# Attention and top-1 experts on one core: token lists by comparisons and matmuls in place of scatters, and the first expert slot begun beside the last attention pair

## The chip, the cores and the metric

The kernel runs on one core of one Trainium2 chip. The metric is the device time of one execution in microseconds; before and after are compared by the median of their runs. The engines are called PE (matmuls), DVE (vector), ACT (scalar), POOL (GpSimd) and SP (its queue issues most of the loads). Each works through its own queue of instructions in the order in which the program issues them.

## The reference, cut to what matters

```python
q_rot, k_rot = (rotate(q), rotate(k))                  # 8 batches, 8 heads, 576 tokens, 64 wide
scores = scale * np.matmul(q_rot, k_rot.transpose(0, 1, 3, 2))
attn = softmax(scores)
x = (attn @ v).transpose(0, 2, 1, 3).reshape(4608, 512)
logits = x @ w_gate
e_idx = np.argmax(logits, axis=1)                      # one of 8 experts for each token
gate_w = softmax(logits)[np.arange(N), e_idx]
eom = 1.0 / (1.0 + np.exp(-(x @ w_output_gate)))
for e in range(8):
    mask = e_idx == e
    h = np.maximum(x[mask] @ w1[e], 0.0)               # 512 x 1024
    out[mask] = gate_w[mask, None] * eom[mask, e, None] * (h @ w2[e])
```

Which token goes to which expert is known only when the attention of the token has been computed, so the kernel makes lists of tokens for each expert as it runs and gathers the rows by them.

## The kernel before, in words

**Attention.** 32 pairs of heads (8 batches, 4 pairs each), 9 steps a pair, 288 steps. In a step (`Attention.step`) PE computes the scores of 128 queries in one of two PSUM tiles (`scores`, lines 432 and 439), DVE takes the row maximum (`peak`, 445), ACT the exponential (`exp`, 454), and one step later DVE transposes it in blocks of 32 (`turn`, 460). Everything else of a pair is issued at fixed steps by the list `EVENTS`: the load of the next pair's q and k on SP (`load`), the rotation on POOL (`mult`, 388, and `add`, 392), the split into a high and a low part on ACT and POOL (364, 372), the value products on PE in four pieces (`values`, 479) in steps 2, 4, 6 and 8 of the next pair, then `evict` on ACT (486 to 488), `back` on PE (494), which turns the rows to tokens and computes the gates' logits, and `divide` on DVE and ACT (502 to 511), which writes a tile `xb` of the batch. So each `evict` (line 486) ends a pair's work on PE.

**Placing a batch.** `place` returns a list of small pieces, issued one a step from step 36b+47 on for batch b. The small arithmetic is on POOL for all batches but the last, for which it is on DVE. The pieces choose the expert (s0 to s8), compute the gate (s9 to s12), store the rows to a DRAM tensor `xd` by SP (s13), compute each token's place in its expert's list by two small matmuls (s14, lines 599 and 600; their PSUM tile is borrowed from the score tiles), and round it to an integer (s17, 612). Then five pieces each issue an indirect DMA from POOL (`scatter`, 616), which writes 128 token numbers, 4 bytes each, to one of five list tensors in DRAM. These five are filled with a large number at the start.

**Tables.** `table0`, `table1` (two tables) turn the counts of tokens into a list of slots; each ends in `slots`, which gathers list rows from the five list tensors by five indirect DMAs on POOL (706), some pieces later takes the minimum of the five on DVE (713), transposes it on PE (717) and rounds it to indices (718). The first table counts the tokens of batches 0 to 5 only. Its pieces begin at `att.done(nb - 3) + 1`; `nplace` is there the length of the last batch's list of pieces, 23, so that step is 251, and the gather falls among batch 5's scatters. `fetch` gathers the rows of slots 0 and 1 (832); its tile shares the buffers of `xb`.

**The passage.** After step 287 the pools of the rotation are closed and the first four weight loads are issued (`begin0`). After one more step the score tiles are closed and two PSUM banks (`ps_x`) take small tiles. The rest of the events up to step 296 follows (the last pair's value products, line 479, and `evict`), then `begin1`: the split of the first weights (`split`, 854 and 856), the transposes of the gathered rows (`turn`, 870 to 873), two more splits. Then the last `back` and `divide`. Only then is the attention's PSUM closed and `ps_m` opened with four tags: `ph0`, `ph1` for the first products, `py0`, `py1` for the second.

**Experts.** 14 slots of 256 tokens and 12 of 128 (`todo`): 5 by the first table, 9 and 12 by the second and third. A slot has eight parts: four times `first` (products with w1, lines 888 and 898) and four times `second` (926). In each, weights six parts ahead are split, weights eight parts ahead are loaded, and two of the pieces `left` are issued: the last batch's placing, merged with the second and third table's. `store` scatters the result (938), `gather` fetches rows (832), both on POOL's queue.

## Time and profile before

| | |
|---|---|
| median of three runs | 1230.01 us (1220.46, 1232.24, 1230.01) |
| the profiled execution | 1221.57 us, its span 1219.8 us |
| granted TensorE clock, mean | 0.924 |
| busy: PE | 1074.2 us, 88% |
| busy: DVE, ACT, POOL | 835.0, 640.2, 597.9 us |
| first `evict` (line 486), last | 54.1 us, 709.2 us |
| indirect scatters of the lists | 40, mean 1040 ns on POOL |

The profile is of one execution. Busy times are sums over the span. A row of a group of instructions has its line, engine and operation, the tile written and the tile read, the shapes and the count, then busy time and mean ns of one, then the idle time of its engine just before, with the instruction that ended it. In the timeline a row has its start, its length, and in brackets the idle time before it with the releaser; "issue" there is time in which the engine waited for nothing that the profile shows. The granted clock is 1.00 at full speed and 0.50 at half.

### The profile page before, as it was taken

Reading aid. Unit: us, or ns where it says so; the run is one execution under the profiler, and the core shown is the slowest. Engines: PE = TensorE matmul, PEld = TensorE weight load, DVE = VectorE, ACT = ScalarE, POOL = GpSimd, SP = SyncE. Lnnn points to the kernel's source line nnn. Section 1 sums busy time; section 2 is a strip of 40 time slices with the busy share of each in tenths; the row PEclk is TensorE's granted clock in tenths of the full one; section 3 lists DMA queues with packets and bytes.
Section 4 is the critical chain, followed back from the end, with each engine's and each line's share of the span. In section 5 each row is a group of like instructions: output and inputs, shape, how many; then the busy total and the mean of one; then the engine's idle time right before and its main releaser. Section 6 shows DMA issues by size and latency. Waiting matters only on the chain.

```text
span 1219.8 us, 34628 instructions
## 1 busy us (share of the span) xinstructions
PE 1074.2 (88%) x14419; PEld 919.9 (75%) x14419; DVE 835.0 (68%) x1335; ACT 640.2 (52%) x1309; POOL 597.9 (49%) x535
## 2 busy tenths in 40 slices
PE   3999985999887888989857879989999999999998
PEld 2877764777766766777646578878988989889986
DVE  6788863876765766767747347655677786786784
ACT  3566642554543544545424245433576675686573
POOL 4676765566774675575554312332154253353242
PEclk9999987988987998878868869989999999999999
DMA  6544486484675675574724647956578788797791
GB/s 206 157 143 134 120 165 80 111 164 112 153 126 86 159 113 140 131 126 110 162 36 79 213 139 210 239 191 214 185 253 301 266 298 278 272 330 263 269 338 40
DMA packets 55713, 216.87 MB, mean 178 GB/s; under 512 B 10337, under 2 KB 11260, under 8 KB 47488
## 3 DMA queue, kind: packets, MB, share of 16 engines
q1 hardware_dynamic: 46432, 194.77, 59.0%
q0 software_dynamic: 8160, 19.03, 4.6%
q8 instruction: 115, 1.88, 0.7%
q10 hardware_dynamic: 960, 0.82, 0.2%
q14 instruction: 46, 0.38, 0.1%
HBM read 195.98 MB, written 20.70 MB: 178 GB/s over the span
## 4 chain that ended last, share of the span: by engine, by line
PE 65%; DVE 12%; issue 9%; DMA 5%; ACT 4%; another core or an unknown queue 2%; POOL 2%; SPq 0%; POOLq 0%; ACTq 0%; DVEq 0%
PE py L926 15%; PE acc L479 14%; PE sc L439 14%; PE ph L898 12%; PE ph L888 4%; DVE pt L460 3%; DVE m L445 3%; PE sc L432 3%; DMA wr<-in_w 2%; PE acc L494 2%; ACT pm L454 2%; DVE wl L856 1%; PE mtp L870 1%; DMA lst<-tok,pi 1%
## 5 line engine op out<-in xcount | busy, mean ns | idle before, releaser
L454 ACT ACTIVATE pm<-sc,m 128x576 f32<-128x576 f32 x288 | 213.2, 740 | 283.1 <-DVE m L445 281.3
L445 DVE TENSOR_REDUCE m<-sc 128x1 f32<-128x576 f32 x288 | 213.7, 742 | 171.2 <-PE sc L439 156.0
L856 DVE TENSOR_TENSOR wl<-wr,wh 128x1024 fp32r<-128x1024 f32 x183 | 252.2, 1389 | 68.3 <-ACT wh L854 66.3
L479 PE MATMUL acc<-pt,v 32*64 32x160 f32 (+1 forms) x9216 | 240.1, 322 | 58.1 <-issue 33.0
L439 PE MATMUL sc<-kh,q 64*128 64x288 f32 x1024 | 239.9, 345 | 54.3 <-ACT pm L454 39.5
L479 PEld LDWEIGHTS acc<-pt,v 32*64 32x64 f32 x9216 | 184.0, 145 | 97.3 <-issue 65.0
L439 PEld LDWEIGHTS sc<-kh,q 64*128 64x128 f32 x1024 | 164.1, 207 | 103.3 <-ACT pm L454 55.8
L460 DVE STREAM_TRANSPOSE pt<-pm 128x576 f32<-128x576 f32 x288 | 220.5, 766 | 12.5 <-ACT pm L454 11.6
L854 ACT CAST wh<-wr 128x1024 fp32r<-128x1024 f32 x208 | 213.1, 1051 | 4.5 <-DMA wr<-in_w 4.4
L926 PE MATMUL py<-wh,ht 128*128 128x512 f32 x640 | 213.8, 399 | 0.0
L898 PE MATMUL ph<-xt,wh 128*128 128x256 f32 x896 | 165.9, 288 | 4.1 <-ACT xb L511 4.1
L388 POOL TENSOR_TENSOR raw<-raw,rt 128x1152 f32<-128x1152 f32 x62 | 164.0, 2646 | 9.4 <-DMA raw<-in_qk 9.3
L898 PEld LDWEIGHTS ph<-xt,wh 128*128 128x128 f32 x896 | 142.9, 195 | 6.1 <-ACT xb L511 4.6
L926 PEld LDWEIGHTS py<-wh,ht 128*128 128x128 f32 x640 | 120.2, 188 | 24.0
L898 PE MATMUL ph<-xt,wl 128*128 128x256 f32 x448 | 128.2, 286 | 0.0
L926 PE MATMUL py<-wl,ht 128*128 128x512 f32 x320 | 125.1, 391 | 0.0
L439 PE MATMUL sc<-kl,q 64*128 64x288 f32 x512 | 118.0, 315 | 0.0
L856 POOL TENSOR_TENSOR wl<-wr,wh 128x1024 fp32r<-128x1024 f32 x25 | 61.1, 2445 | 109.4 <-ACT wh L854 95.5
L439 PEld LDWEIGHTS sc<-kl,q 64*128 64x128 f32 x512 | 92.3, 210 | 0.0
L392 POOL TENSOR_TENSOR raw<-raw 128x576 f32<-128x576 f32 x62 | 87.8, 1416 | 3.2
L372 POOL TENSOR_TENSOR kl<-raw,kh 128x576 fp32r<-128x576 f32 x31 | 44.0, 1418 | 92.2 <-ACT kh L364 92.1
L898 PEld LDWEIGHTS ph<-xt,wl 128*128 128x128 f32 x448 | 87.2, 195 | 0.0
(208 smaller groups left out, 1303.0 us busy)
## 6 DMA issues: line engine op xcount, KB each, us to landing
wr<-in_w SPq DMA_DIRECT2D x208, 512.0 KB
v<-in_v SPq DMA_DIRECT2D x128, 288.0 KB
raw<-in_qk SPq DMA_DIRECT2D x31, 1152.0 KB
xd<-xb SPq DMA_DIRECT2D x8, 1026.0 KB
raw<-in_qk SPq DMA_DIRECT2D x2, 576.0 KB
xd<-xb SPq DMA_DIRECT2D x8, 128.2 KB
lst<-stage SPq DMA_DIRECT2D x5, 144.0 KB
lst<-tok,pi POOLq DMA_INDIRECT x40
```

Source lines behind the costliest of these rows:

```text
L388: self.eng(eng).tensor_tensor(out=rv, in0=rv, in1=self.rt[:, 2 * t:2 * t + 2, x], op=ALU.mult)
L392: self.eng(eng).tensor_tensor(out=r[:, 2 * t, x], in0=r[:, 2 * t, x], in1=r[:, 2 * t + 1, x], op=ALU.add)
L439: nc.tensor.matmul(ps[:, a, :HS], self.q[r, w, c * P:c * P + P], mov[r, a * HS:a * HS + HS], start=(n == 0), stop=(n == 2))
L445: nc.vector.tensor_reduce(self.m[i], ps[:, :, :HS], axis=AX.XY, op=ALU.max, negate=True)
L454: nc.scalar.activation(pe.rearrange("p (a b) -> p a b", a=2), self.ps[i][:, :, :HS], AF.Exp, bias=self.m[i], scale=1.0, accum_out=self.z[: ...
L460: self.nc.vector.transpose(out=self.pt[:, st[0] + 5 * st[1] if st else 4, :], in_=self.pc.pop(i))
L479: nc.tensor.matmul(self.acc[h * D:h * D + D, a, o:o + 32 * n], self.v[r, h, j, :], self.pt[r, u:u + n, 32 * j:32 * j + 32], start=(j == 0) ...
L854: self.nc.scalar.copy(wh, r)
L856: eng.tensor_tensor(out=wl, in0=r, in1=wh.bitcast(F32), op=ALU.subtract)
L888: nc.tensor.matmul(ph[:, 0, :], st[:, dc, 0:P], mv[:, dc, :], start=(n == 0), stop=(n == 11))
L898: nc.tensor.matmul(ph[:, f, :], st[:, dc, fs], mv[:, dc, :], start=(n == 0), stop=(n == 11))
L926: self.nc.tensor.matmul(py[h], st[:, f, hs], mv, start=(f == 0 and n == 0), stop=(f == 7 and n == 2))
```

## The change

The five list tensors, the 40 scatters and the initial fill go. A table `lists` of 128 by 288 stays in SBUF. For each batch the place of a token is divided into a row (shift by 7, s18) and a column (s19). For each group of 128 tokens (`ones(c)`), DVE compares the row number with 288 constants (a bf16 tile `ro`, 128x288), and POOL (DVE for the last batch) compares the column with 128 constants, twice, and multiplies by the two parts of the token number plus one (`pl`, two of 128x128 in bf16). Ten matmuls (s20) add up pl-transposed times ro in a small PSUM tile, and DVE adds the result to `lists`. When a table is due, `turned` transposes `lists` on PE in three parts, copies them on ACT and writes them to DRAM from ACT's queue; `slots` gathers once from there, and 0 (no token) is turned into a large number by two DVE operations in place of the minimum.

The pieces of a batch that isn't the last are put at steps of their own, 39 of them: s14 at 18 (phase 2 of the nine steps, in which a piece of value products is issued) in place of 25 (phase 0), the store s13 at 26 in place of 22, `ones` at 31 to 35, s20 at 38 (phase 4). `nplace` is now that length, so that the first table begins at step 267, and `fetch` is issued 18 steps later, in a tile of its own. The last batch's pieces stand ahead of the second table's and are not merged with them; the waits between a gather and its use are 5 pieces.

The first products of a slot get a PSUM pool of their own (`ps_h`), opened where the score tiles were. The splits of weights 0 to 2 are issued after step 289's events, and after step 296's events the row transposes of slot 0 and the first products of parts 0 and 1 (`products`), ahead of the last `back` and `divide`. The tile `bd` moves to another pool.

```diff
@@ -35,6 +35,8 @@
...
+MID = 144.0
@@ -76,10 +78,10 @@
...
-    tok = p + 128.0 * np.arange(NCH)[None, :]
...
-    parts = [e8, mask, tok, eb, sl, tri, one]
+    row = np.tile(np.arange(E * list_rows(nb) // P) - MID, (P, 1))
+    parts = [e8, mask, p + 1.0, eb, sl, tri, one, row]
@@ -131,9 +133,9 @@
...
-    nl = E * list_rows(nb)
-    lst = [dpool.tile([nl, 1], F32, name=f"lst{c}") for c in range(NCH)]
+    nl = E * list_rows(nb) // P
+    lst = [dpool.tile([nl, P], F32, name=f"lst{c}") for c in range(2)]
@@ -150,9 +152,11 @@
...
-    zero, big = stage[:, nst:nst + 256], stage[:, nst + 256:nst + 256 + nl // P]
+    row = cpool.tile([P, nl], BF16, name="row")
+    lists = cpool.tile([P, nl], F32, name="lists")
+    zero = stage[:, nst:nst + 256]
     nc.vector.memset(zero, 0.0)
-    nc.vector.memset(big, BIG)
@@ -162,18 +166,18 @@
...
-        for l in lst:
-            nc.sync.dma_start(out=l.rearrange("(p n) o -> p (n o)", p=P), in_=big)
-    att = Attention(tc, nb, pools, cc, ident, ii, first, trib, oneb, cnt, zero, qk, v, xd, lst)
+        nc.vector.tensor_copy(row, sc(C_ROW))
+        nc.vector.memset(lists, 0.0)
+    att = Attention(tc, nb, pools, cc, ident, ii, first, trib, oneb, cnt, zero, qk, v, xd, row, lists)
     n0 = slot_counts(nb)[0]
-    moe = Moe(tc, nb, (px, px2, small), cc, ident, cnt, w, xd, lst, out)
+    moe = Moe(tc, nb, (px, px2, small), cc, ident, cnt, w, xd, lists, lst, out)
...
-        for k, f in enumerate(pieces(moe.table0(), 21)):
+        for k, f in enumerate(pieces(moe.table0(), 18)):
             att.at(g + k, 2, f)
-        att.at(att.done(nb - 2) - att.nplace + 22, 2, moe.fetch)
+        att.at(g + 18, 2, moe.fetch)
@@ -185,22 +189,28 @@
...
+    moe.ph = pool(ctx, "ps_h", 1, space=PSUM, side="right", reuse_waits="tile")
...
+        att.rest(lambda g: g <= att.G + 1)
+        for u in range(3):
+            moe.split(u)
         att.rest(lambda g: g <= att.G + 8)
-        moe.begin1()
+        for h in range(2):
+            moe.turn(0, h)
+        for j in range(2):
+            moe.products(0, j)
...
-        a, b, n = att.last, pieces(moe.table1(), 60), len(att.last) - NCH
-        left = a[:n] + [lambda f=f, g=g: (f(), g()) for f, g in zip(a[n:], b)] + b[NCH:]
+        left = att.last + pieces(moe.table1(), 60)
@@ -231,7 +241,7 @@
...
-            o = (pp1.tile([P, 2, P], F32R, name=f"bd{i}"), px.tile([P, 2 * NCH], F32, name=f"z{i}"),
+            o = (px.tile([P, 2, P], F32R, name=f"bd{i}"), px.tile([P, 2 * NCH], F32, name=f"z{i}"),
@@ -267,11 +277,11 @@
...
-                fs = place(tc, (px, px2, small), b, NT, cc, trib, oneb, cnt, xbs, xd, lst)
-                self.nplace = len(fs)
+                fs = place(tc, (px, px2, small), b, NT, cc, trib, oneb, cnt, xbs, xd, row, lists)
...
+                    self.nplace = len(fs)
@@ -565,6 +575,8 @@
     def s8():
...
+    def add0():
@@ -589,7 +601,8 @@
...
-        V.tensor_scalar(new("tok", [P, NCH]), cc(C_TOK), float(b * S), None, op0=ALU.add)
+    def base():
@@ -611,39 +624,63 @@
     def s17():
...
-    def scatter(c):
-        m = QR if c == 4 else P
-        nc.gpsimd.indirect_dma_start(
-            out=lst[c][:, :], out_offset=bass.IndirectOffsetOnAxis(ap=T["pi"][:m, c:c + 1], axis=0),
-            in_=T["tok"][:m, c:c + 1], in_offset=None, bounds_check=E * list_rows(NT // S) - 1, oob_is_err=False)
+    def s18():
+        nc.vector.tensor_scalar(new("hi", [P, NCH], I32), T["pi"], 7, None, op0=ALU.logical_shift_right)
+    def s19():
+        V.tensor_copy(new("hr", [P, NCH]), T["hi"])
+        V.tensor_scalar(T["hr"], T["hr"], -MID, None, op0=ALU.add)
+        lo = new("lo", [P, NCH])
+        V.tensor_scalar(lo, T["hr"], -float(P), -(P + 1) * MID, op0=ALU.mult, op1=ALU.add)
+        tt(out=lo, in0=lo, in1=T["po"], op=ALU.add)
+    def ones(c):
+        if c == 0:
+            new("ro", [P, NCH, lists.shape[1]], BF16)
+            new("pl", [P, NCH, 2, P], BF16)
+        nc.vector.tensor_scalar(T["ro"][:, c, :], row, T["hr"][:, c:c + 1], None, op0=ALU.is_equal)
+        for i, x in enumerate((cc(C_P1), float(b * S + c * P))):
+            V.tensor_scalar(T["pl"][:, c, i, :], row[:, 0:P], T["lo"][:, c:c + 1], x, op0=ALU.is_equal, op1=ALU.mult)
+    def s20():
+        T["ls"] = small.tile(f"ls{b}").rearrange("p a b -> p (a b)")[:, 0:lists.shape[1]]
+        for c in range(NCH):
+            m = QR if c == 4 else P
+            for i in range(2):
+                nc.tensor.matmul(T["ls"], T["pl"][0:m, c, i, :], T["ro"][0:m, c, :], start=(c == 0 and i == 0),
+                                 stop=(c == 4 and i == 1))
+        nc.vector.tensor_tensor(out=lists, in0=T["ls"], in1=lists, op=ALU.add)
     def both(f, c):
...
-        fs = [s0, s1, s2, s3, s4, s5, s6, s7, s8, both(s9, 1), both(s10, 2), both(s11, 3), both(s12, 4), s13, s14, s15, s16, s17]
-    else:
-        no = lambda: None
-        fs = [s0, s1, s2, no, no, s3, no, no, s4, s5, s6, s7, no, no, s8, both(s9, 1), both(s10, 2), both(s11, 3),
-              lambda: add(4), no, no, s12, s13, no, no, s14, s15, no, no, s16, s17]
+        return [s0, s1, s2, s3, s4, s5, s6, s7, lambda: (s8(), add0()), both(s9, 1), both(s10, 2), both(s11, 3), both(s12, 4),
+                lambda: (s13(), base()), s14, s15, s16, s17, s18, s19] + [lambda c=c: ones(c) for c in range(NCH)] + [s20]
+    fs = {0: s0, 1: s1, 2: s2, 5: s3, 8: s4, 10: s5, 11: s6, 12: s7, 13: add0, 14: both(lambda: add(1), 2),
+          15: both(lambda: add(3), 4), 16: s8, 17: base, 18: s14, 19: s9, 20: s15, 21: lambda: (s10(), s11()), 23: s16, 24: s12,
+          25: s17, 26: s13, 28: s18, 29: s19, 38: s20}
     for c in range(NCH):
-        fs += [lambda c=c: scatter(c)]
-    return fs
+        fs[31 + c] = lambda c=c: ones(c)
+    return [fs.get(k, lambda: None) for k in range(39)]
...
-    def __init__(self, tc, nb, pools, cc, ident, cnt, w, xd, lst, out):
+    def __init__(self, tc, nb, pools, cc, ident, cnt, w, xd, lists, lst, out):
...
-        self.cc, self.ident, self.cnt, self.w, self.xd, self.lst, self.out = cc, ident, cnt, w, xd, lst, out
+        self.cc, self.ident, self.cnt, self.w, self.xd, self.lists, self.lst, self.out = cc, ident, cnt, w, xd, lists, lst, out
...
-        self.wr, self.wp, self.xt, self.ht, self.gss, self.pys, self.hrs, self.regs = ({} for _ in range(8))
+        self.wr, self.wp, self.xt, self.ht, self.gss, self.pys, self.hrs, self.regs, self.phs = ({} for _ in range(9))
@@ -696,27 +733,42 @@
...
-        tks = [t([m, P], f"{n}tk{c}") for c in range(NCH)]
-        for tk in tks:
-            self.nc.gpsimd.memset(tk, BIG)
+        tk, g = t([m, P], f"{n}tk"), t([m, P], f"{n}g")
+        self.nc.gpsimd.memset(tk, 0.0)
...
-        for l, tk in zip(self.lst, tks):
-            self.nc.gpsimd.indirect_dma_start(
-                out=tk, out_offset=None, in_=l.rearrange("(r c) o -> r (c o)", c=P),
-                in_offset=bass.IndirectOffsetOnAxis(ap=ri[0:m, :], axis=0), bounds_check=E * self.rows - 1, oob_is_err=False)
+        self.nc.gpsimd.indirect_dma_start(
+            out=tk, out_offset=None, in_=self.rowsd[:, :],
+            in_offset=bass.IndirectOffsetOnAxis(ap=ri[0:m, :], axis=0), bounds_check=E * self.rows - 1, oob_is_err=False)
...
-        tk = tks[0]
-        for o in tks[1:]:
-            V.tensor_tensor(out=tk, in0=tk, in1=o, op=ALU.min)
+        V.tensor_scalar(g, tk, 0.5, BIG, op0=ALU.is_le, op1=ALU.mult)
+        V.scalar_tensor_tensor(out=tk, in0=tk, scalar=-1.0, in1=g, op0=ALU.add, op1=ALU.add)
...
+    def turned(self, k):
+        nc, N = self.nc, self.lists.shape[1]
+        tr, lt = self.small.tile(f"ltr{k}"), self.t([P, -(-N // P), P], f"lt{k}")
+        d = self.rowsd = self.lst[k]
+        for g in range(0, N, P):
+            nc.tensor.transpose(out=tr[0:min(P, N - g), g // P, :], in_=self.lists[:, g:min(N, g + P)], identity=self.ident)
+        yield
+        n, m = N // P, N % P
+        if n:
+            nc.scalar.copy(lt[:, 0:n, :], tr[:, 0:n, :])
+            nc.scalar.dma_start(out=d[0:n * P, :].rearrange("(g p) c -> p g c", p=P), in_=lt[:, 0:n, :])
+        if m:
+            nc.scalar.copy(lt[0:m, n, :], tr[0:m, n, :])
+            nc.scalar.dma_start(out=d[n * P:N, :], in_=lt[0:m, n, :])
+        yield
@@ -745,10 +798,11 @@
...
-        yield from self.slots(0, 2 * self.n0, end, dl, None, 2, 10)
+        yield from self.slots(0, 2 * self.n0, end, dl, None, 2, 5)
     def table1(self):
         V, t = self.nc.vector, self.t
+        yield from self.turned(1)
@@ -780,7 +834,7 @@
...
-            yield from self.slots(2, 2 * self.n2, end, d2, g2[:, 0:1], 2, 16)
+            yield from self.slots(2, 2 * self.n2, end, d2, g2[:, 0:1], 2, 5)
@@ -795,7 +849,7 @@
...
-        yield from self.slots(1, self.n1, e1, d1, g1[:, 0:1], 1, 8)
+        yield from self.slots(1, self.n1, e1, d1, g1[:, 0:1], 1, 5)
@@ -805,7 +859,7 @@
     def fetch(self):
-        xg = self.px2.tile([P, NCH, XW], F32, tag="xb", name="xg")
+        xg = self.px2.tile([P, 4, XW], F32, tag="xg", name="xg", bufs=1)
@@ -872,23 +926,17 @@ and @@ -897,6 +945,21 @@
+    def products(self, s, j):
...
+        xth, xtl = self.xt[s]
...
+        ph = self.phs[s, j] = self.ph.tile([P, 2, SLOT], F32, tag=f"ph{j % 2}", name=f"ph{s}_{j}{self.nm}")
...
+    def first(self, s, j):
...
+        if (s, j) not in self.phs:
+            self.products(s, j)
+        ph = self.phs.pop((s, j))
```

More of the change, by code (lines that the diff above doesn't have):

```diff
@@ L51 @@
 TURN = 1
-C_E8, C_MASK, C_TOK, C_EB, C_SL, C_TRI, C_ONE = range(7)
+C_E8, C_MASK, C_P1, C_EB, C_SL, C_TRI, C_ONE, C_ROW = range(8)
 def list_rows(nb):
@@ L218, with __init__ @@
 class Attention:
-    def __init__(self, tc, nb, pools, cc, ident, ii, first, trib, oneb, cnt, zero, qk, v, xd, lst):
+    def __init__(self, tc, nb, pools, cc, ident, ii, first, trib, oneb, cnt, zero, qk, v, xd, row, lists):
         nc = tc.nc
@@ L512, in divide, with place @@
                                  scale=rz[0:QR, 8 + h:9 + h])
-def place(tc, pools, b, NT, cc, trib, oneb, cnt, xbs, xd, lst):
+def place(tc, pools, b, NT, cc, trib, oneb, cnt, xbs, xd, row, lists):
     nc = tc.nc
@@ L735, in table0 @@
         V, t = self.nc.vector, self.t
+        yield from self.turned(0)
         fn, fi = self.padded("fn"), t([P, E], "fi", I32)
@@ L873, in turn @@
         V.tensor_tensor(out=xtl[:, :, hs], in0=tp, in1=xth.bitcast(F32)[:, :, hs], op=ALU.subtract)
-    def first(self, s, j):
+    def products(self, s, j):
         nc = self.nc
-        fl = lambda a: a.rearrange("p a b -> p (a b)")
-        if j == 0:
-            self.ht[s] = [self.buf(f"ht{i}", 0, 1, 0, [P, 8, SLOT], F32R, f"ht{i}_{s}{self.nm}") for i in range(2)]
-        (xth, xtl), (hth, htl) = self.xt[s], self.ht[s]
+        xth, xtl = self.xt[s]
         wh, wl = (a.rearrange("p (d f) -> p d f", f=256) for a in self.wp.pop(8 * s + j))
-        js = slice(2 * j, 2 * j + 2)
-        ph = self.pm.tile([P, 2, SLOT], F32, tag=f"ph{j % 2}", name=f"ph{s}_{j}{self.nm}")
+        ph = self.phs[s, j] = self.ph.tile([P, 2, SLOT], F32, tag=f"ph{j % 2}", name=f"ph{s}_{j}{self.nm}")
         if self.todo[s][0] == 1:
@@ L889, in first @@
                     n += 1
-            hr = self.hrs[s, j] = self.buf("hr", j, 3, 0, [P, 2, P], F32, f"hr{s}_{j}{self.nm}")
-            nc.scalar.activation(fl(hr), ph[:, 0, :], AF.Relu)
             return
@@ L899, in first @@
                     n += 1
+    def first(self, s, j):
+        nc = self.nc
+        fl = lambda a: a.rearrange("p a b -> p (a b)")
+        if j == 0:
+            self.ht[s] = [self.buf(f"ht{i}", 0, 1, 0, [P, 8, SLOT], F32R, f"ht{i}_{s}{self.nm}") for i in range(2)]
+        hth, htl = self.ht[s]
+        js = slice(2 * j, 2 * j + 2)
+        if (s, j) not in self.phs:
+            self.products(s, j)
+        ph = self.phs.pop((s, j))
+        if self.todo[s][0] == 1:
+            hr = self.hrs[s, j] = self.buf("hr", j, 3, 0, [P, 2, P], F32, f"hr{s}_{j}{self.nm}")
+            nc.scalar.activation(fl(hr), ph[:, 0, :], AF.Relu)
+            return
         nc.scalar.activation(fl(hth[:, js, :]), fl(ph), AF.Relu)
```

## The prediction

> **What bounds the kernel now.** I first cut the span at the copies that end an attention pair (line 486, 32 of them) and read the windows view: length, then busy time of PE, PEld, DVE, ACT and POOL with their instruction counts, granted clock, DMA share, GB/s.
>
> ```profile
> 54.10:121.60 67.50, 63.02 (x1409) 52.57 (x1408) 56.51 (x98) 41.59 (x111) 43.60 (x27) 1.00 0.51 142
> 121.60:682.10 560.50, 472.73 (x9165) 387.14 (x9164) 384.76 (x708) 270.86 (x715) 333.84 (x346) 0.87 0.59 120
> 682.10:717.50 35.40, 22.64 (x316) 14.62 (x317) 8.21 (x19) 6.86 (x18) 9.55 (x11) 0.70 0.56 184
> 717.50:1219.80 502.30, 482.90 (x3132) 437.78 (x3132) 346.71 (x457) 298.96 (x423) 182.43 (x126) 0.98 0.74 246
> ```
>
> The first row is four pairs in which no batch is placed yet: PE busy 63.0 of 67.5 us at clock 1.00. The second is 26 pairs with the placing of batches 0 to 5 in them, PE waits more and the clock is 0.87. The third is the passage to the experts, the fourth the experts, where PE has 482.9 of 502.3 us and little is to be had. One batch's four pairs, cut apart in the same view:
>
> ```profile
> 155.60:179.10 23.50, 19.75 (x359) 15.91 (x358) 14.51 (x28) 10.43 (x30) 13.33 (x11) 0.85 0.94 199
> 179.10:211.70 32.60, 19.86 (x347) 15.87 (x347) 15.12 (x26) 10.58 (x30) 19.00 (x16) 0.78 0.68 71
> 211.70:231.00 19.30, 18.84 (x356) 15.76 (x357) 14.23 (x27) 10.43 (x28) 8.68 (x13) 0.84 0.45 125
> 231.00:247.80 16.80, 15.60 (x353) 13.01 (x352) 14.03 (x25) 10.42 (x30) 11.96 (x15) 1.00 0.34 87
> ```
>
> The fourth is an undisturbed pair, 16.8 us. The other three, where the rank product and then the five scatters fall, are 6.7, 15.8 and 2.5 us longer. Over the 26 pairs the excess is 560.5 - 26 x 16.8 = 123.7 us. That is what the change can act on. The waits view of PE over the 26 pairs (sum, times, longest) says how it is lost, and over the experts what the tables cost there:
>
> ```profile
> PE acc L479 <- issue: 30.5, 21, 8.0
> PE sc L439 <- ACT pm L454: 29.8, 26, 11.9
> PE 0tr L717 <- DVE 0tk L713: 4.1, 1, 4.1
> ...
> PE 2tr L717 <- DVE 2tk L713: 8.4, 1, 8.4
> PE 1tr L717 <- DVE 1tk L713: 2.6, 1, 2.6
> ```
>
> "issue" is PE standing with nothing to wait for. The long ones come behind scatters. The timeline, with the idle time before a row in brackets, has the three kinds of loss:
>
> ```profile
> 156.22 0.18 PE L600 MATMUL rk<-ohb,trib 128*128 128x40 bf16 x1
> 158.03 0.53 PE L439 MATMUL sc<-kh,q 64*128 64x288 f32 x2 [1.62 <-ACT pm L454]
> 159.01 1.29 PE L494 MATMUL acc<-ii,ac 128*128 128x160 f32 x7
> 160.00:163.00 3.00, 3.00 (x15) 1.96 (x14) 1.99 (x7) 1.40 (x5) 0.05 (x1) 0.50 1.00 161
> ...
> 196.97 1.38 PE L479 MATMUL acc<-pt,v 32*64 32x160 f32 x32 [7.97 <-issue]
> 636.36 0.84 PE L439 MATMUL sc<-kh,q 64*128 64x288 f32 x2 [11.95 <-ACT pm L454]
> 621.89 0.94 POOL L706 DMA_INDIRECT 0tk<-lst,0ri  x1 [5.95 <-DMA lst<-tok,pi]
> 628.71 0.93 POOL L706 DMA_INDIRECT 0tk<-lst,0ri  x1 [5.88 <-DMA lst<-tok,pi]
> ```
>
> First: the rank product borrows one of the two score banks, in a step with no value product to run meanwhile; PE is empty for 1.62 us, and soon after the clock stands at 0.50 (the windows row). Second: PE stands for 7.97 us while little but scatter traffic has happened. Third: the first table's gathers sit in POOL's queue, each waiting some 6 us for a scatter of batch 5 to land; POOL's rope behind them is late, and PE loses 11.95 us.
>
> **The change part by part. Rank product (s14).** It moves to a step in which 72 value products stand ready behind it, 1.6 us of work by the 80 that take 1.64 us in the fence below. I take 0.7 us a batch for what is left (0.3 to 2), 6 x 0.7 = 4 us. Without that cover it costs the 1.62 us and the slow clock again, 6.7 us a batch.
>
> [...]
>
> **Scatters.** Thirty of the forty, those of batches 0 to 5, stand in the 26 pairs. All forty go, with `tok`, and nothing on POOL issues a DMA there any more but the rows' gathers. I book the whole rest of the 123.7 us to them and to the table that waits for them, because the undisturbed pair has the same loads and the same rope.
>
> **The lists by comparison.** New for each batch: one small shift (DVE), four small POOL operations, five comparisons of 128x288 on DVE, ten of 128x128 on POOL, ten matmuls of 288 columns, one addition of 128x288. No such operation is in the trace; the nearest rows:
>
> ```profile
> L546 POOL TENSOR_SCALAR sc<-dd 128x40 f32<-128x40 f32 x7 | 2.3, 330 | 0.0
> L579 POOL TENSOR_SCALAR eg<-eg 128x5 f32<-128x5 f32 x7 | 1.7, 248 | 4.2 <-ACT eg L573 4.2
> L388 POOL TENSOR_TENSOR raw<-raw,rt 128x1152 f32<-128x1152 f32 x62 | 164.0, 2646 | 9.4 <-DMA raw<-in_qk 9.3
> L155 DVE MEMSET stage<- 128x288 f32 x1 | 0.3, 298 | 0.0
> 583.66 2.54 DVE L739 TENSOR_SCALAR fi<-fi 128x8 int32<-128x8 int32 x1
> 583.56 2.60 POOL L388 TENSOR_TENSOR raw<-raw,rt 128x1152 f32<-128x1152 f32 x1
> ```
>
> POOL: 330 - 248 = 82 ns for 35 elements, 2.3 ns each, so 128 elements take 248 + 123 x 2.3 = 0.53 us, ten 5.3 us. POOL is busy 43.6 / 4 = 10.9 us of an undisturbed pair; 16.2 with these, which just fits. DVE: 0.3 us each by the memset row, five 1.5 us, in steps that DVE sets (56.5 of 67.5 us). But the last two rows show a shift of 8 elements that takes 2.54 us, as long as the POOL operation that began before it. A comparison can stand so too: none (0) up to 2.65 us. With POOL busy two thirds of the time and half an operation left on average, I take 0.65 us, five 3.3 us. PE: the six score products from 158.03 to 159.01 take 0.98 us, 0.16 each, so ten take 1.6 us; the addition 0.4 us by the memset row; 0.7 us for the borrowed bank, beside the next pair's second piece of value products. With 1.6 us for a clock that falls now and then: 1.5 + 3.3 + 1.6 + 0.4 + 0.7 + 1.6 = 9 us a batch. Low end 3 us (no stands, work under PE); high end 18 us (five whole stands of 2.65 us and the rest). Queued behind: on DVE the `peak` and `turn` of the step, on which the exponential and so the scores wait; on PE, behind the ten matmuls, the next scores. I take the middle because the trace has both free and held small operations. 6 x 9 = 54 us (18 to 108).
>
> [...]
>
> **The first table** begins 16 steps later, when batch 5's list is complete; it adds three transposes, two ACT copies and two DMAs on ACT's queue (behind them wait exponentials), and has one gather for five. Its gather comes 11 steps after the list's write, so POOL no longer stands. The 11.95 and 4.1 us go; DVE's small operations (the shift's 2.54 us again) and the transpose stay: 8.5 us (4 to 15, the upper end being near what the two idles cost now).
>
> Attention: 123.7 - 4 - 54 - 8.5 = 57 us gained. Ends: 123.7 - 2 - 18 - 4 = 100, and 123.7 - 12 - 108 - 15 = -11, a loss.
>
> **The passage.** PE and POOL there:
>
> ```profile
> 686.56 1.64 PE L479 MATMUL acc<-pt,v 32*64 32x160 f32 x80 [1.74 <-ACT xb L511]
> 692.88 6.73 PE L479 MATMUL acc<-pt,v 32*64 32x160 f32 x73 [0.30 <-issue]
> 701.38 4.04 PE L479 MATMUL acc<-pt,v 32*64 32x128 f32 x104 [0.35 <-issue]
> 710.14 3.23 PE L494 MATMUL acc<-ii,ac 128*128 128x160 f32 x10 [3.33 <-ACT ac L488]
> 717.50 0.80 PE L898 MATMUL ph<-xt,wh 128*128 128x256 f32 x2 [4.13 <-ACT xb L511]
> ...
> 687.80 1.16 POOL L832 DMA_INDIRECT xg<-xd,0idx  x1 [9.16 <-DMA xd<-xb]
> 699.44 0.92 POOL L616 DMA_INDIRECT lst<-tok,pi  x1 [0.30 <-issue]
> ```
>
> The last pair's 288 value products should take 288 / 80 x 1.64 = 5.9 us; they take 686.56 to 705.42, 18.9, and they are slow from the first row gather (687.80) until the last scatter (700.36). Nine indirect DMAs lie in that time. The change takes away five and lets the four gathers start earlier, since their tile no longer shares a buffer with the one that waited 9.16 us for its store. 18.9 - 5.9 = 13 us is my value; the low end is 4 us, if gathers still overlap. The first two products of slot 0 now come ahead of the last pair's `back`, on banks of their own, and fill the 3.33 + 4.13 us; they need gathered rows, turned, and two split weights, loaded before the last step, so I take 5 us of 7.5 (2 to 8). Together 18 us (6 to 21). The store of batch 6 moves past the four weight loads on SP; nobody before the second table waits for it.
>
> **The experts.** The second and third tables lose four of five gathers but their waits shrink from 16 and 8 pieces to 5, some three matmul steps; the last batch adds 15 comparisons on DVE (15 x 0.3 = 4.5 us, under PE's matmuls, which DVE with 346.7 of 502.3 us can bear), ten matmuls and three transposes on PE, about 2 us. Of 8.4 + 2.6 = 11 us I take 9 as gained, less 2: 7 us (-4 to 10). At the start a table row is added and five list fills go: 0, within 1 us, under the first loads; uncovered, the two added DVE operations are 0.6 us.
>
> Sum: 57 + 18 + 7 = 82 us, from the profiled execution's 1221.6 us to 1139.6. That execution lies 8.4 us under the median of the three runs, 1230.0; I add half of it: **1143 us**. About 1% is what a measurement of this kernel can tell from no change.
>
> **The rivals.** [...] Every comparison waits for a whole rope operation, 18 us a batch: 54 us more, 1197. For it, the 2.54 us shift; against it, the undisturbed pair, which has small DVE operations beside the same rope and is not slowed. *Cheap lists.* 3 us a batch, all under PE: 36 us less, 1107. For it, POOL's 5.9 us to spare per pair; against it, DVE's 14 of 16.8. *The passage stays slow* because the four gathers, not the scatters, hold PE: 6 us for 18, 1155. For it, the slowness begins with the first gather. *The scatters are innocent*, PE's stands have another source: then of 123.7 only the rank's 6 x 6.7 = 40 and the table's 16 us go, 67 us stay, and the passage too: 1143 + 67 + 12 = 1222, no change that can be told. Against it, undisturbed pairs have none. *POOL becomes the bound* (the other side): if a POOL comparison costs not 0.53 us but L388's 2.65, the pair with the lists needs 10.9 + 26.5 us of POOL in 16.8, the rope is 20.6 us late in each of six batches, 124 us: 1267. It is slower than before from 10.9 + 10x - 16.8 > 14.5, x about 2.0 us. Against it, the 0.33 us of the 40-element row.
>
> **How the numbers follow.** Forecast 0.53; ports 0.15; passage 0.12; cheap lists 0.11; innocent 0.05; POOL 0.04. The first four, 0.91, are faster by over 1% (I say 0.90), the fifth within 1% (0.06), the last slower (0.04). The range, 1102 to 1197, holds the forecast, the cheap lists and the slow passage, and ends at the ports' case.
>
> **What would show it.** Right: pairs of 17 to 19 us where 23.5 and 32.6 stand, one pair in four about 9 us over 16.8; no "issue" wait of several us between 121 and 650; clock near 0.95 there; POOL comparisons near 0.5 us; DVE's list comparisons with a mean of 0.5 to 1.2 us; the last pair's value products in about 6 us, the first expert product ahead of `back`; 2tr with a wait under 3 us. Wrong: stands of 2 us and more in DVE's comparisons, "issue" waits that remain without scatters, a pair over 30 us, or value products slow beside the four gathers.

## The result, and the profile after

The changed kernel takes 1181.35 us (median of four runs, 1174.63 to 1187.67), the kernel before 1231.12 (four runs): a ratio of 0.961, 95% interval 0.954 to 0.968. That is 50 us less, inside the range forecast and on the side forecast, but 87 us less were forecast. The profiled execution, the slowest of the four, took 1187.67 us, its span 1185.9, 33.9 us under the span before.

The same cuts as before: up to the fifth evict, the 26 pairs to the thirty-first, the passage to the first expert product, the experts (length, busy time of PE, PEld, DVE, ACT, POOL, clock, DMA share, GB/s):

```profile
54.30:121.90 67.60, 62.99 (x1409) 52.55 (x1408) 56.51 (x98) 41.68 (x111) 43.66 (x27) 1.00 0.51 142
121.90:652.00 530.10, 474.54 (x9228) 390.85 (x9227) 404.20 (x751) 271.20 (x717) 351.81 (x390) 0.88 0.49 131
652.00:674.20 22.20, 11.32 (x307) 9.30 (x307) 7.13 (x16) 6.20 (x15) 8.60 (x15) 0.77 0.75 221
674.20:1185.90 511.70, 489.76 (x3165) 440.94 (x3165) 353.17 (x481) 299.62 (x427) 167.51 (x105) 0.98 0.71 241
```

The 26 pairs lost 30.4 us of their 560.5. Their clock is 0.88, where I expected 0.95. Batch 0's four pairs, cut as before:

```profile
156.70:180.40 23.70, 20.12 (x356) 16.14 (x354) 16.25 (x29) 10.36 (x29) 19.05 (x21) 0.78 0.71 163
180.40:202.10 21.70, 21.55 (x361) 17.80 (x362) 16.19 (x30) 10.49 (x29) 12.84 (x13) 0.77 0.36 100
202.10:219.00 16.90, 15.66 (x353) 13.07 (x352) 14.01 (x26) 10.35 (x29) 11.44 (x15) 1.00 0.49 140
219.00:239.30 20.30, 18.81 (x357) 15.65 (x357) 15.15 (x29) 10.54 (x31) 13.32 (x16) 0.83 0.44 121
```

The pair behind the scatters went from 32.6 to 21.7 us. The pair ahead of it still takes 23.7, though the rank product is no longer in it. PE's waits in the 26 pairs, and below the dots those in the experts:

```profile
PE acc L489 <- ACT xb L521: 25.0, 23, 1.9
PE acc L489 <- issue: 14.6, 8, 3.9
PE sc L449 <- ACT pm L464: 11.8, 23, 2.0
...
PE ph L946 <- DVE ht L964: 4.4, 1, 4.4
PE ls L653 <- DVE pl L645: 3.0, 2, 1.9
```

Stands without a releaser ahead of value products fell from 30.5 to 14.6 us, but there should have been none: no scatter is left. The table's waits of 8.4 and 2.6 us in the experts are gone, and new ones have come, 4.4 us in one and 3.0 us in two.

Span by span: 26 pairs -30.4; thirty-first evict to last evict 27.1 to 20.1, -7.0; last evict to the end of slot 0's 96 first products 22.5 to 26.1, +3.6; from there to the last matmul 482.4 to 475.9, -6.5; last matmul to the end 5.7 to 11.8, +6.1; ahead of the 26 pairs +0.3. Together -33.9.

### The profile page after: what moved, and what is told of

The parts are those of the page before. It is cut to its first block, busy times and chain, and to the rows that moved or that the text cites. A ratio compares the mean times of both kernels' runs of the same rounds, so it can differ in the third digit from the quotient of the medians.

```text
span 1185.9 us, 34808 instructions
## 1 busy us (share of the span) xinstructions
PE 1071.1 (90%) x14505; PEld 921.0 (78%) x14505; DVE 860.0 (73%) x1399; ACT 640.6 (54%) x1313; POOL 600.1 (51%) x562
## 4 chain that ended last, share of the span: by engine, by line
PE 71%; DVE 14%; issue 8%; ACT 4%; DMA 2%; POOL 0%; ACTq 0%; POOLq 0%; DVEq 0%
PE py L989 17%; PE acc L489 15%; PE sc L449 15%; PE ph L946 13%; DVE pt L470 4%; PE ph L938 4%; DVE m L455 4%; PE sc L442 3%; ACT pm L464 2%; PE acc L504 2%; PE mtp L924 1%; ACT xb L521 1%; DVE xb L512 1%; DVE wl L910 1%; ACT wh L908 1%
## 5 line engine op out<-in xcount | busy, mean ns | idle before, releaser
L489 PE MATMUL acc<-pt,v 32*64 32x160 f32 (+1 forms) x9216 | 225.8, 321 | 52.3 <-ACT xb L521 30.6
L489 PEld LDWEIGHTS acc<-pt,v 32*64 32x64 f32 x9216 | 179.8, 144 | 82.4 <-issue 43.7
L989 PEld LDWEIGHTS py<-wh,ht 128*128 128x128 f32 x640 | 120.9, 189 | 25.1 <-issue 0.2
```

Of the source, the lines that this page charges most:

```text
L489: nc.tensor.matmul(self.acc[h * D:h * D + D, a, o:o + 32 * n], self.v[r, h, j, :], self.pt[r, u:u + n, 32 * j:32 * j + 32], start=(j == 0) ...
L989: self.nc.tensor.matmul(py[h], st[:, f, hs], mv, start=(f == 0 and n == 0), stop=(f == 7 and n == 2))
```

## The experiments

The figure is mostly the length of the 26 pairs, fifth evict to thirty-first. It has a scatter of its own: two further kernels below with the changed kernel's attention untouched had 515.2 and 513.9 us in their profiled executions, where the changed kernel had 530.1. Chips differ too: the kernel before took 1254.5, 1219.7 and 1231.7 us on the three chips of the experiments, so ratios are each to the kernel before on the same chip. That doesn't make ratios from two chips comparable to better than about 3%: the changed kernels have nearly the same undisturbed pairs (16.7 to 17.1 us, the one with fillers aside) and the same experts (475.8 to 478.8 us from the end of slot 0's first products to the last matmul) on all three, so what varies seems to lie mostly in the kernel before. Lengths of single pairs are the safer measure.

Theory one was that the list work is what remains, theory two that it is the falling clock, theory three that it is the store of a batch's rows, which the change moves from piece 22 to piece 26.

**The list work left out.**

```diff
-          25: s17, 26: s13, 28: s18, 29: s19, 38: s20}
+          25: s17, 26: s13, 28: s18, 29: s19, 38: lambda: None}
-        fs[31 + c] = lambda c=c: ones(c)
+        fs[31 + c] = lambda: None
-        nc.vector.memset(lists, 0.0)
+        nc.vector.memset(lists, 1.0)
```

> The changed kernel, with the list work of batches 0 to 6 left out: no comparisons on DVE and POOL, none of their ten matmuls and no addition; the table starts at one, so every slot but the last batch's tokens works on token 0, and only the time up to the last pair's evict is read. The figure is the length of the 26 pairs from the fifth evict to the thirty-first, 560.5 us before and 530.1 us changed. Theory one (the lists' own work on DVE, POOL and PE is what remains, at the 9 us a batch that were forecast or more): 476 us or less. Theory two (what remains is the clock, which falls to half for 4 to 20 us whenever PE has stood a little longer, whoever made it stand): the falls that list work sets off go, the others stay, about 495 to 505 us. Theory three (PE's stands without a releaser, where the store of the rows meets the next pair's loads): 515 us or more.

```profile
124.10:615.10 491.00, 441.62 (x9168) 364.54 (x9166) 382.08 (x715) 271.51 (x716) 306.52 (x331) 0.93 0.55 142
```

491.0 us, ratio 0.915 (0.909 to 0.921). Without list work the six pairs with the store in them still take 18.3 to 21.6 us, 20 us together over undisturbed ones. The list work of six batches costs 39 us against the profiled execution, 23 to 24 against the other two: 4 to 6.5 us a batch, under the 9 forecast. Theory one falls: 54 us over undisturbed pairs are left without any list work. The number lies just under where theory two put it.

**PE kept busy where it waits in every pair.**

```diff
+    def fill(self, trib, oneb, n):
+        for _ in range(n):
+            self.nc.tensor.matmul(self.acc[:, 2, 400:512], oneb, trib[:, 0:112], start=True, stop=True, skip_group_check=True)
```

> The changed kernel with ten small matmuls (128x112, bf16) in each pair, into a part of the value products' PSUM that nothing reads, in the place where PE waits some 1.1 us of every pair for the pair before to be divided. Theory two: seven of the sixteen falls of the clock in the 26 pairs begin at that regular wait; with PE busy there they go, 3.4 us each, and the 26 pairs take about 505 us at a clock of 0.95 or more. Theories one and three: the falls come from the list work and from the store, so the 26 pairs take 525 to 535 us, or a little longer for the added matmuls.

538.0 us, ratio 0.958 (0.952 to 0.965), no different from the changed kernel. But this edit doesn't do what it was meant to do. The fillers (line 510) write the value products' PSUM tile, so they wait for the same division, and PE stands there as long as it did ahead of the value products (25.0 us in 23 waits in the changed kernel); the fillers only come on top. Theory two was not put to the test by this run. Undisturbed pairs took 17.4 to 18.0 us, and the clock fell even in the first pairs, which were at 1.00 before:

```profile
PE acc L510 <- ACT xb L526: 27.3, 25, 2.0
...
54.00:121.00 67.00, 62.30 (x1355) 52.24 (x1359) 52.39 (x93) 38.47 (x101) 39.00 (x24) 0.97 0.48 132
```

**The store moved off the loads.**

```diff
-          25: s17, 26: s13, 28: s18, 29: s19, 38: s20}
+          25: s17, 30: s13, 28: s18, 29: s19, 38: s20}
```

> The changed kernel with the store of a batch's rows four steps later, past the next pair's loads. Theory three: the stands without a releaser (14.6 us in the 26 pairs) and the falls of the clock behind them go, 530 to about 505 us. Theories one and two: within 8 us of 530, the stands shorter at most.

506.4 us, theory three's number; ratio 0.926 (0.921 to 0.932), where the kernel with fillers has 0.958 on the same chip. The stands without a releaser ahead of value products are down to 1.1 us, from 14.6, and the pair that took 23.7 us takes 18.4 at a full clock; the one behind it, with the list work, takes 24.0:

```profile
PE acc L489 <- ACT xb L521: 32.7, 26, 3.3
PE sc L449 <- ACT pm L464: 12.0, 30, 1.8
PE sc L449 <- issue: 2.1, 1, 2.1
...
PE acc L489 <- issue: 1.1, 2, 0.9
...
124.00:630.40 506.40, 455.49 (x9228) 374.67 (x9226) 406.07 (x751) 271.12 (x716) 351.33 (x390) 0.93 0.53 137
...
158.70:177.10 18.40, 16.43 (x356) 13.53 (x355) 15.70 (x28) 10.39 (x30) 13.60 (x16) 1.00 0.44 103
177.10:201.10 24.00, 22.00 (x360) 17.67 (x361) 18.51 (x30) 10.47 (x30) 19.87 (x18) 0.79 0.79 171
```

This holds in every batch: the six pairs with the store in them took 20.2 to 25.1 us in the changed kernel, 19.6 to 24.2 in the two kernels with the same attention, and take 18.3 or 18.4 here, 19 to 26 us less in all. The six pairs behind them grew, from 21.5 to 22.3 us on average to 23.5. What the store costs the 26 pairs on balance is therefore 24 us against the changed kernel's profiled execution, but only 7.5 to 9 us against the two others (515.2 and 513.9).

What the store meets is seen on SP's queue. First the changed kernel:

```profile
160.99 0.40 SPq L602 DMA_DIRECT2D xd<-xb  x1
161.45 0.52 SPq L603 DMA_DIRECT2D xd<-xb  x1
162.06 3.62 SPq L393 DMA_DIRECT2D v<-in_v  x4
169.31 0.35 SPq L387 DMA_DIRECT2D raw<-in_qk  x1
```

Then the one with the store moved:

```profile
158.29 2.76 SPq L393 DMA_DIRECT2D v<-in_v  x4
174.10 0.40 SPq L602 DMA_DIRECT2D xd<-xb  x1
174.54 0.53 SPq L603 DMA_DIRECT2D xd<-xb  x1
175.16 1.27 SPq L387 DMA_DIRECT2D raw<-in_qk  x1
```

In the changed kernel the four loads of v stand in the queue behind the store: they start 5.4 us behind the pair's evict (156.7), without the store 0.4 us ahead of it (158.7). Store, v and the next q and k lie closer together there. A stand of 2.62 us ended at 486.07; the DMA view of 483 to 487 us has the engines' whole share taken (105.5%) and, among it, one packet of instructions:

```profile
q1 hardware_dynamic: 258, 1.04, 105.5%
q8 instruction: 1, 0.02, 1.6%
```

Seven of the eight longest stands in the 26 pairs end 2.5 to 2.9 us after a packet of that queue began, 73 of which come in these 530 us. Of the 15 stands without a releaser of over 1 us in the 26 pairs of this profile and of that of the kernel before, 11 end 2.2 to 3.1 us after one, where an eighth would by chance. The 7.97 us stand of the kernel before ends 6.0 us after a packet that took 4.9 us; the median there is 1.2. So PE probably stands for its next instructions here, and they come late where data fill the engines. That is my reading of the coincidence, and no run here moves the instruction packets; the effect of the store's place is shown.

**The rank product without cover,** first with the store where the change has it:

```diff
-  ... 17: base, 18: s14, 19: s9, 20: s15, 21: lambda: (s10(), s11()), 23: s16, 24: s12,
-          25: s17, 26: s13, 28: s18, 29: s19, 38: s20}
+  ... 17: base, 19: s9, 21: lambda: (s10(), s11()), 24: s12,
+          25: s14, 26: lambda: (s15(), s13()), 27: s16, 28: s17, 29: s18, 30: s19, 38: s20}
```

> The changed kernel with the rank product back in the step without value products, and the five steps behind it packed closer. As forecast, the cover is worth 6 us a batch: 530 to about 566 us for the 26 pairs. Theory two: without cover PE stands 1.6 us and the clock falls for certain where it fell in half of the pairs before: 3.4 + 1.6 less 1.7, some 3 us a batch, about 548 us. If the place of the rank product doesn't matter: 525 to 535 us.

545.5 us, ratio 0.964 (0.956 to 0.972). And then with the store off the loads (`30: lambda: (s19(), s13())`):

> The changed kernel with the store moved off the loads and the rank product back in the step without value products: the price of the cover alone, with the store out of the way. As forecast 6 us a batch, 36 us on 506: 542 us. By the runs so far (15 us between the same two places with the store on the loads) 2 to 3 us a batch: about 520 us.

```profile
121.50:647.90 526.40, 469.83 (x9228) 386.56 (x9226) 400.24 (x748) 271.06 (x716) 350.97 (x388) 0.90 0.51 132
```

526.4 us against 506.4, so by these two profiles the cover is worth 20 / 6 = 3.3 us a batch, not the 6 forecast. With the store on the loads it is 15 us against the changed kernel's profile and 30 to 32 against the two others, 2.6 to 5.3 us a batch. The ratios, 0.957 (0.951 to 0.963) against 0.926, are of two chips and differ by more than these lengths do; they don't settle it.

**The kernel before without scatters.**

```diff
-        fs += [lambda c=c: scatter(c)]
+        fs += [(lambda c=c: scatter(c)) if last else (lambda: None)]
```

> The kernel before, with the thirty-five scatters of batches 0 to 6 left out and the lists filled with zero, so that all slots work on token 0; only the time up to the last evict is read. As forecast (the scatters and the table that waits for them hold all of the excess but the rank product's): the 26 pairs shrink from 560.5 us to about 437 + 6 x 6.7 = 477 us, table included some 485, and PE's stands without a releaser, 30.5 us, go. If the scatters are innocent of those stands (the store of the rows beside the loads makes them, as the run with the store moved suggests for the changed kernel): 30 us of such stands remain and the pairs take 530 us or more.

```profile
122.00:603.80 481.80, 432.61 (x9165) 358.52 (x9163) 385.09 (x708) 270.58 (x715) 303.05 (x316) 0.95 0.54 140
```

481.8 us, ratio 0.930 (0.921 to 0.940, two runs). The scatters, with the table that waits for them, held 78.7 us; 75 were forecast (83.5 less 8.5 for what stays of the table). Stands without a releaser ahead of value products fell from 30.5 to 4.7 us. The scatters were not innocent, and this step of the forecast was right to 4 us.

**The kernel before with its first table later.** `nplace` is set from the other batches' lists of pieces, so the table starts at step 264.

> The kernel before with one part of the change alone: the first table begins 13 steps later, behind batch 5's scatters. Theory: its gathers no longer wait on POOL for scatters to land, so the stands of 11.95 and 4.1 us go, the rest stays: 16 us less, a ratio near 0.987. Rival: the table's late start only moves its waits onto the gather of the rows and the passage: within 5 us of before.

Ratio 0.990 (0.985 to 0.995), 12 us. The sum is near the 16 us of the theory, the place is not: the 26 pairs took 556.8 us, only 4 less. Their stands of 11.95 and 4.1 us went, and stands behind scatters were longer in this execution (41.7 us). 11.9 us came in the passage, 27.1 to 15.2. The last pair's value products there:

```profile
684.79 4.45 PE L479 MATMUL acc<-pt,v 32*64 32x160 f32 x215 [1.74 <-ACT xb L511]
693.00 2.54 PE L479 MATMUL acc<-pt,v 32*64 32x128 f32 x73 [3.76 <-issue]
```

215 of them run at full pace in 4.45 us, beside the four row gathers (683.2 to 688.3 on POOL). So the four gathers don't slow the value products here. The scatters, which follow from 689.7 to 695.8, are not cleared: the stand of 3.76 us and the last 73, which take 2.54 us in place of 1.5, lie beside them.

**The kernel before without scatters, with the store's piece later.** Piece 22 keeps the arithmetic; the two DMAs go to piece 26.

> The kernel before without the scatters of batches 0 to 6 (481.8 us for the 26 pairs, lists filled with zero, so that all slots work on token 0) and with the store of a batch's rows four steps later, on the step where the changed kernel has it, beside the next pair's loads. If the store beside the loads makes PE stand, whatever else is in the kernel: stands without a releaser rise from 4.7 us to 12 or more, and the 26 pairs take about 500 us. If the store only harms beside the new list work: 478 to 486 us.

476.2 us, ratio 0.917 (0.911 to 0.924, two runs). This edit did not test what it was meant to. SP runs ahead of the steps and waits only for data, which here were ready as early as ever: the first row is the store in the kernel before, the second in this one.

```profile
154.06 0.40 SPq L590 DMA_DIRECT2D xd<-xb  x1
```

```profile
154.03 0.40 SPq L596 DMA_DIRECT2D xd<-xb  x1
```

What changed is that the load of q and k no longer stands behind it. In the changed kernel the store's data themselves come later (the gate's last steps were moved too), which holds v behind it.

**The comparisons moved away from the rope,** with the store moved as above:

```diff
-    for c in range(NCH):
-        fs[31 + c] = lambda c=c: ones(c)
+    for k, cs in ((36, (0, 1)), (37, (2, 3)), (38, (4,))):
+        fs[k] = lambda cs=cs: [ones(c) for c in cs]
```

> The changed kernel with the store four steps later (as in the run before, 506.4 us for the 26 pairs) and the comparisons moved from the five steps beside the rope to three steps in which POOL has little of it (two, two and one a step), the matmuls two steps later. If DVE's stands behind POOL's rope are what the list work costs (in the run with the store moved a comparison takes up to 2.8 us against 0.25 to 0.3 undisturbed), the mean of a comparison falls to under 0.5 us, the pairs of 21 to 24.7 us behind each batch go to 18 or 19, and the 26 pairs take 485 to 492 us. Rival (the ten matmuls, the addition and the clock that falls behind them are the cost, wherever the comparisons stand): 500 to 510 us.

```profile
122.30:615.30 493.00, 442.13 (x9229) 363.58 (x9227) 390.31 (x752) 271.16 (x717) 349.94 (x388) 0.95 0.54 140
```

493.0 us, ratio 0.933 (0.927 to 0.938), on another chip than the 0.926 above. Comparisons (minimum, median, maximum in ns), in the changed kernel and in this one:

```profile
L643 DVE TENSOR_SCALAR ro<-row,hr x40: 246/300/2505, 171.7 to 728.9; 128x288 bf16<-128x288 bf16 x40
```

```profile
L643 DVE TENSOR_SCALAR ro<-row,hr x40: 240/294/428, 180.2 to 686.0; 128x288 bf16<-128x288 bf16 x40
```

The long ones are gone, and the 26 pairs went from 506.4 to 493.0, 1 us short of the forecast's range. Yet the pairs behind batches took 20.0 to 25.6 us, not 18 or 19: stands without a releaser came back, 13.5 us in six, the longest 4.0, all of them in those pairs. The program is the same for PE but for two steps' shift of ten matmuls and the borrowed bank. If the stands are late fetches, which pair is hit depends on where data meet them, and moving any work moves that; this is not shown.

What such a long comparison is, in the kernel with only the store moved, on DVE and on POOL:

```profile
178.51 2.66 DVE L643 TENSOR_SCALAR ro<-row,hr 128x288 bf16<-128x288 bf16 x1
```

```profile
178.47 2.61 POOL L398 TENSOR_TENSOR raw<-raw,rt 128x1152 f32<-128x1152 f32 x1
```

A comparison that takes 0.25 us when nothing holds it takes 2.66 here and ends 0.09 us after the rope operation that began 0.04 us ahead of it. In the changed kernel's profile 14 of the 40 comparisons take over 0.43 us, and each of the 14 ends 0.09 us after an operation of the rope (lines 398 and 402) that began ahead of it. Away from the rope the longest took 0.43 us, the 428 ns above. What in the chip holds them is not shown by any run.

**The passage.** As before the change, the splits and row transposes behind step 296 and the first products behind the last division:

```diff
-        att.rest(lambda g: g <= att.G + 1)
-        for u in range(3):
-            moe.split(u)
         att.rest(lambda g: g <= att.G + 8)
-        for h in range(2):
-            moe.turn(0, h)
-        for j in range(2):
-            moe.products(0, j)
+        moe.begin1()
```

> The changed kernel with the passage as before: splits and row transposes behind step 296's events, the first products behind the last division (still on banks of their own). As forecast, the products ahead of the division are worth 5 us, so this one is 5 us slower than the changed kernel. Rival, from the profile after: they are worth nothing, since the third product then waits 4.4 us for the first one's bank, whose activation stands on ACT behind the division and three weight splits; from the last evict to the end of slot 0's first products 22 to 24 us as before, against 26 us, and the time within 3 us of the changed kernel.

Ratio 0.952 (0.945 to 0.960) against 0.961 (0.954 to 0.968): not slower, as far as two chips can be compared. Last evict to the end of slot 0's first products: 20.8 us against 26.1, so the 5 us forecast aren't there. The profile after shows why it isn't worth more to put them ahead, on ACT:

```profile
685.40 2.93 ACT L908 CAST wh<-wr 128x1024 fp32r<-128x1024 f32 x3
688.23 0.59 ACT L963 ACTIVATE ht<-ph 128x512 fp32r<-128x512 f32 x1
```

The first product's bank is free only when its activation has run, and that stands behind the division's last scaling and three weight splits; PE waits 4.4 us for it. So I moved splits 3 to 5 behind the first two activations (`run`, `slot`):

> The changed kernel with the splits of weights 3 to 5 issued behind the first and second activation of slot 0 in place of ahead of them. If the bank is what the third product waits for, its wait of 4.4 us shrinks to under 1 us and the whole is 3 to 4 us shorter than the changed kernel. Rival: the wait only moves on to the later weights, which are now split later, and nothing is gained.

Ratio 0.958 (0.950 to 0.967). The wait is now 4.2 us in two parts, and 24.9 us stand in place of 26.1. The rival holds: it has moved on. Last, the passage as before on top of the two moves of the attention:

> The same with the passage as before the change, the first products behind the last division. From the profiles of the other runs (from the last evict to the end of slot 0's first products 20.8 us so, 24.4 to 26.1 us with the products ahead) 4 us less than the one above. Rival: what was gained there lies in that one run's clock, and the two are equal within 2 us.

1146.91 us against 1147.22, ratios 0.932 and 0.933: equal, as the rival has it. From thirty-first evict to the end of the first products 42.2 us against 40.0. The order of the passage is worth nothing that can be told, in either direction.

Three of the kernels that leave nothing out have intervals wholly below the changed kernel's: the two with store and comparisons moved (1147 us where the kernel before takes 1231.7) and the one with the store alone (0.926).

## Why the prediction was right or wrong

Right in sign and for the main reason: the scatters and the table behind them held the largest loss, 78.7 us where 75 were reckoned, and the experts gave 6.5 us where 7 were. The second agreement may be luck: the kernel before with its first table later takes 477.8 us there, 4.6 less than the kernel before, with the old tables and their waits of 6.9 and 1.3 us still in it. The forecast is wrong in size by 37 us of 87.

**The step that failed** is a sentence on the moved store: "nobody before the second table waits for it". It asked who waits for the store, for batch 6 alone, and not what stands behind it on SP or what it meets on the DMA engines. Moved four pieces on, with its data, it holds the next v loads: 530.1 against 506.4 us in the 26 pairs, stands of 14.6 against 1.1 us, 27 us of the span of the profiled executions. Against the two other kernels with this attention (stands of 15.7 and 14.6 us) it is 7.5 to 9 us of the 26 pairs, so the step is certain and its size is not. This was priced at zero. The prediction had named the sign of it: "issue" waits that remain without scatters. They did remain. Which part does it, the late v loads or the transfers that overlap, was not tried apart.

**List work:** 9 us a batch forecast, 4 to 6.5 measured. The term for held comparisons, 0.65 us each, doesn't follow from the row beside it: two thirds of half of 2.65 us is 0.88. No run shows the 1.6 us a batch for a clock that falls now and then; what the runs show is the clock of the 26 pairs, 0.88 with the list work, 0.93 without it and 0.95 with store and comparisons moved. The parts: DVE's comparisons up to 2.5 us, as bounded, beside 0.30 at the median; POOL's took more than the 0.53 us from the 40-element rows:

```profile
L645 POOL TENSOR_SCALAR pl<-row,lo,ct x35: 782/794/837, 171.9 to 669.1; 128x128 bf16<-128x128 bf16 x35
L645 POOL TENSOR_SCALAR pl<-row,lo x35: 701/712/727, 172.7 to 670.0; 128x128 bf16<-128x128 bf16 x35
```

0.79 and 0.71, far below the 2.0 us from which POOL would have decided. The rival in which every comparison waits for a whole rope operation, the one that the forecast's chances call the ports', was right in kind at a smaller price: taking the waits away was worth 13.4 us on balance, with 12 us of new stands in that kernel, so their own price may be anything from 13 to some 26 us. That ports are what holds the comparisons no run shows.

**Rank product:** its pair cost 6.7 us more, and I took the whole as the price of the missing cover. The cover is worth 2.6 to 5.3 us a batch; that pair also has loads in it. What was left under cover was sized well: with store and comparisons moved, the pair with the rank product takes 17.7 us in every batch, 0.9 over an undisturbed one, where 0.7 was forecast.

**First table:** with no list work the last three pairs ahead of the thirty-first evict still take 615.1 - 546.0 = 69.1 us, 18.7 over undisturbed ones, some 16 more than the same three pairs of other batches; 8.5 were forecast. Which of its parts costs this was not tried.

**The passage:** 18 us forecast, 7.0 - 3.6 = 3.4 measured. The 13 us were put on nine indirect DMAs; in the kernel with the first table later 215 value products run at full pace beside the four gathers, 4.45 us, when no stand falls there. With the scatters gone PE stood 6.49 us there without a releaser, ending at 666.31, while seven weight loads were queued (653.38 to 662.18 on SP). And the 5 us for the first products ahead of `back` went into the wait for the bank: the product's bank and its activation were not followed to the next product.

**The end:** 6.1 us that nobody forecast, below.

## What to carry to other kernels

Price a moved DMA by what stands behind it in its queue and by the transfers it will overlap, not only by who waits for its data; an issuing engine that runs ahead of the schedule, as SP does here, sets the real time by the data, not by the place in the program (the store at 154.06 us from piece 22, at 154.03 from piece 26). When PE is nearly full, a stand with no releaser is a place to look at the DMA engines' load and at the instruction packets. Work that begins earlier must be followed to the release of its buffers, or the wait reappears one buffer later.

## What the runs showed of the hardware

PE's clock fell after a wait of only 1.12 us in the changed kernel: the windows row of 219.00 to 239.30 has 0.83, and the longest wait in it is this one, in the timeline of PE:

```profile
224.06 2.31 PE L489 MATMUL acc<-pt,v 32*64 32x160 f32 x76 [1.12 <-ACT xb L521]
```

From 224.56 to 231.38 us the clock is 0.50. The 76 value products behind the wait take 2.31 us, all 80 of them 2.58, where 80 took 1.64 at a clock of 1.00 (207.03 in this profile). A wait of the same length, 1.12 us up to 143.96, left the clock of its pair (138.90 to 156.70) at 1.00. So the length of the wait alone doesn't decide it.

The traces say much of what makes one such wait count and another not. Eight profiles have rows of 1 us in the windows view: before, changed, without list work, with fillers, store moved, both of the rank product, comparisons moved. In their 26 pairs the clock falls to 0.50 114 times, each time for 3.41 us or a whole multiple of it, up to six, and within one profile the falls lie whole multiples of 3.41 us apart. With the 26 pairs of the kernel before and of the changed one cut into such stretches, those at full clock in which PE was idle for less than a quarter saw a fall at their end in 1 of 178 cases, those in which it was idle for 40% or more in 21 of 25, those between in 14 of 36. A wait of 1.12 us is a third of a stretch. So in these two profiles it counts, or doesn't, mostly by where it lies in its stretch and what else stands there; four stretches with 40% or more had no fall, and these stay unexplained.

The end of the program grew: POOL's last drain took 2.4 us before, 6.9 changed, 8.2 in the kernel before without scatters (rows in that order, the last number of the three).

```profile
L1033 POOLq DRAIN  x3: 46/107/2399, 1216.5 to 1219.5; - x3
```

```profile
L1096 POOLq DRAIN  x3: 46/107/6852, 1178.2 to 1185.6; - x3
```

```profile
L1033 POOLq DRAIN  x3: 46/107/8241, 1123.8 to 1132.9; - x3
```

The two that lack the scatters of batches 0 to 6 have the long one. From the last matmul to the end the changed kernel takes 11.8 us, the kernel before 5.7. Its cause stays open.
